# Dense work placed under the attention's exps by a build-time list schedule, with exps that carry no shift

## The chip, the cores and the metric

The kernel is one transformer block on one core of one Trainium2 chip. The metric is device time in microseconds of that core, the median of several executions. The engines are PE (matmul; PEld is its weight loading), ACT (activations), DVE (vector), POOL (GpSimd) and SP, which issues the DMAs. The program gives each engine its own instruction list in a fixed order, with semaphores between the lists.

## The reference

The block works on 2048 tokens of width 1024, in bf16: layer norm, attention with 32 heads of width 32, output projection, residual; then layer norm, a feed-forward layer of width 3584 with GELU, residual.

```python
def _A_ref(x, wqkv, wo):                       # attention
    q, k, v = ...(x @ wqkv)                    # 32 heads, Dh = 32
    p = softmax(einsum("bhqd,bhkd->bhqk", q, k) * Dh ** -0.5)
    return einsum("bhqk,bhkd->bhqd", p, v)... @ wo

def _B_ref(x, w1, b1, w2, b2):                 # feed-forward
    return gelu(x @ w1 + b1) @ w2 + b2         # tanh approximation

h  = x + _A_ref(layernorm(x), wqkv, wo)
h2 = h + _B_ref(layernorm(h), w1, b1, w2, b2)
```

## The kernel before

Three stages run one after the other: all projections; all attention; then, per chunk of 512 tokens, output projection, layer norm and feed-forward. In attention the scores of two heads, 128 keys and 512 queries form one "half unit": two matmuls of contraction 32 (row tiles of the PE array) into a 128x1024 score buffer in PSUM, and one exp of that buffer on ACT. For two half units together, four column tiles of PV and four of the denominator follow.

```python
NSTP = 2                                     # two score buffers
def stage_A(hu):                             # QK: two of four row tiles
    for j in range(2):
        hl = 2 * pr + j
        pe(matmul(sT[:, s, j, :], KT[32*hl:32*hl+32, g, kt*P:(kt+1)*P],
                  QT[32*hl:32*hl+32, g, qc*512:(qc+1)*512],
                  tile_position=(32 * hl, 0)), ...)
def stage_B(hu):                             # exp with a per-partition bias
    act(activation(PT[:, ps], sT[:, s], ACT.Exp, bias=biasm[:, g, qc:qc+1], scale=SCALE))
def stage_C(hu1):                            # four PV, then four denominator column tiles
    ...
for hu in range(NHU):                        # 1024 half units
    if hu + LA < NHU:
        stage_A(hu + LA); stage_B(hu + LA)
    if hu % 2 == 1:
        stage_C(hu); ...
# ... only then, chunk by chunk:
# output projection, layer norm, feed-forward (GELU by sigmoid on ACT)
```

`biasm` is an upper bound of the scores from row norms of Q and K: 64 squares on DVE, 64 matmuls with ones, 64 reductions. It keeps the exp's argument small.

Of the kernel before, what the change touches and what calls it, by code (L numbers as in the profile page):

```python
# [6 lines left out]
dt = mybir.dt  # L7
# [6 lines left out]


class Flow:

    def __init__(self, sem, eng, step=1):
        self.sem = sem
        self.eng = eng  # L20
        self.step = step
        self.count = 0
        self.pending = False

    def horizon(self):
        return self.value() + (self.step if self.pending else 0)

    def value(self):
        return self.count * self.step


class Buf:

    __slots__ = ("w", "r")

    def __init__(self):
        self.w = None
        self.r = {}


class Task:
    __slots__ = ("fn", "waits", "flow", "inc")

    def __init__(self, fn, waits, flow, inc):
        self.fn = fn
        self.waits = waits
        self.flow = flow
        self.inc = inc


class Plan:
    def __init__(self):
        self.tasks = {}
        self.main_flow = {}
        self.all_flows = []
        self.regions = []

    def register_flow(self, flow):
        self.all_flows.append(flow)
        return flow  # L60

    def track(self, space, lo, hi, bufs):
        deps = {}

        def merge(dep):
            if dep is None:
                return
            f, v = dep
            if deps.get(f, 0) < v:
                deps[f] = v  # L70

        for (sp, l, h, obufs) in self.regions:
            if sp == space and l < hi and lo < h:
                for ob in obufs:
                    merge(ob.w)
                    for f, v in ob.r.items():
                        merge((f, v))
        for b in bufs:
            for f, v in deps.items():
                if b.r.get(f, 0) < v:  # L80
                    b.r[f] = v
        self.regions.append((space, lo, hi, bufs))

    def add_engine(self, eng, flow):
        self.tasks[eng] = []
        self.main_flow[eng] = flow
        self.register_flow(flow)

    def task(self, eng, fn, reads=(), writes=(), flow=None, inc=True):
        if flow is None:  # L90
            flow = self.main_flow[eng]
        assert flow.eng == eng
        waits = {}

        def need(dep):
            if dep is None:
                return
            f, v = dep
            if v <= 0:
                return  # L100
            cur = waits.get(f)
            if cur is None or cur < v:
                waits[f] = v

        for b in reads:
            need(b.w)
        for b in writes:
            need(b.w)
            for f, v in b.r.items():
                need((f, v))  # L110
        if flow in waits and waits[flow] > flow.value():
            raise RuntimeError("same-engine dependency on a not-yet-incremented task; add inc=True")
        if inc:
            flow.count += 1
            flow.pending = False
            val = flow.value()
        else:
            flow.pending = True
            val = flow.value() + flow.step
        t = Task(fn, waits, flow if inc else None, inc)  # L120
        self.tasks[eng].append(t)
        for b in writes:
            b.w = (flow, val)
            b.r = {}
        for b in reads:
            old = b.r.get(flow)
            if old is None or old < val:
                b.r[flow] = val
        return t

    def emit(self, eng, eng_obj):
        waited = {}
        for t in self.tasks[eng]:
            for f, v in t.waits.items():
                if waited.get(f, 0) >= v:
                    continue
                eng_obj.wait_ge(f.sem, v)
                waited[f] = v
            ins = t.fn(eng_obj)
            if t.inc:  # L140
                ins.then_inc(t.flow.sem, t.flow.step)


class LNTemps:

    def __init__(self, SB, T, pfx, nslots, nbn, tiles=4):
        tq = tiles
        B = [Buf() for _ in range(nslots)]
        self.B = B

        def mk(name, shape, dtype):
            h, _ = SB(T, pfx + name, shape, dtype, bufs=B)
            return h

        self.stats = mk("stats", [P, nslots, tq, nbn * 6], dt.float32)
        self.mv = mk("mv", [P, nslots, tq, 2], dt.float32)
        self.mvb = mk("mvb", [P, nslots, tq, 2], dt.bfloat16)
        self.mvr = mk("mvr", [P, nslots, tq, 2], dt.float32)
        self.nm = mk("nm", [P, nslots, tq, 1], dt.float32)
        self.tb = mk("tb", [P, nslots, tq, 1], dt.bfloat16)  # L160
        self.y0 = mk("y0", [P, nslots, tq, 1], dt.float32)
        self.r0 = mk("r0", [P, nslots, tq, 1], dt.float32)
        self.q0 = mk("q0", [P, nslots, tq, 1], dt.float32)
        self.y1 = mk("y1", [P, nslots, tq, 1], dt.float32)
        self.denb = mk("denb", [P, nslots, tq, 1], dt.bfloat16)
        self.rden = mk("rden", [P, nslots, tq, 1], dt.float32)


class LanePool:

    def __init__(self, flows):
        self.flows = flows
        self.tokens = [Buf() for _ in flows]
        self.i = 0

    def next(self):
        k = self.i % len(self.flows)
        self.i += 1
        return self.flows[k], self.tokens[k]


def build_kernel(nc, A_x, A_wqkv, A_wo, B_w1, B_b1, B_w2, B_b2, out):
# [3 lines left out]
    H = D // DH  # L186
    assert D % P == 0 and S % 512 == 0 and F % P == 0 and H * DH == D
    NT = S // P
    NCH = S // 512
    DC = D // P  # L190
    G = DC
    FC = F // P
    OB = min(512, D)
    NVB = D // OB
    assert D % OB == 0
# [6 lines left out]
    out2 = out[0]  # L202

    plan = Plan()
    es = ExitStack()
    with es:
        T = es.enter_context

        def sem(name):
            return T(nc.semaphore(name))  # L210

        fpe = Flow(sem("f_pe"), E.PE)
        fact = Flow(sem("f_act"), E.Activation)
        fdve = Flow(sem("f_dve"), E.DVE)
        fpool = Flow(sem("f_pool"), E.Pool)
        fsp_dummy = Flow(sem("f_sp"), E.SP)
        plan.add_engine(E.PE, fpe)
        plan.add_engine(E.Activation, fact)
        plan.add_engine(E.DVE, fdve)
        plan.add_engine(E.Pool, fpool)  # L220
        plan.add_engine(E.SP, fsp_dummy)
        lanes_x = LanePool([plan.register_flow(Flow(sem(f"f_dx{i}"), E.SP, 16)) for i in range(3)])
        lanes_w = LanePool([plan.register_flow(Flow(sem(f"f_dw{i}"), E.SP, 16)) for i in range(6)])
        lanes_m = LanePool([plan.register_flow(Flow(sem(f"f_dm{i}"), E.SP, 16)) for i in range(2)])
        lanes_o = LanePool([plan.register_flow(Flow(sem(f"f_do{i}"), E.SP, 16)) for i in range(4)])

        def _flatten(x):
            if isinstance(x, Buf):
                return [x]
            out_ = []  # L230
            for y in x:
                out_ += _flatten(y)
            return out_

        def _mkbufs(shape):
            if shape is None:
                return Buf()
            if isinstance(shape, int):
                return [Buf() for _ in range(shape)]
            n, rest = shape[0], (shape[1] if len(shape) == 2 else shape[1:])  # L240
            return [_mkbufs(rest) for _ in range(n)]

        def SB(T_, name, shape, dtype, bufshape=None, bufs=None):
            h = T_(nc.sbuf_tensor(name, shape, dtype))
            m = nc.lookup_mloc(h)
            nbytes = mybir.dt.size(dtype)
            for d_ in shape[1:]:
                nbytes *= d_
            if bufs is None:
                bufs = _mkbufs(bufshape)  # L250
            plan.track("SB", m.addr, m.addr + nbytes, _flatten(bufs))
            return h, bufs

        def PSM(T_, name, shape, dtype, bufshape=None):
            h = T_(nc.psum_tensor(name, shape, dtype))
            m = nc.lookup_mloc(h)
            nbytes = mybir.dt.size(dtype)
            for d_ in shape[1:]:
                nbytes *= d_
            nbanks = (nbytes + 2047) // 2048  # L260
# [236 lines left out]
        def projections(tc, mid_hook=None):  # L497
# [12 lines left out]
            for jv in range(NVB):  # L510
                jb = (2 * D) // WBLK + jv
                s = load_wblock(jb)
                if jv == 0:
                    flush_tail()
# [381 lines left out]
```

## Time and profile before

| | before |
|---|---|
| median | 1880.46 us (3 runs); 1883.87 us with the run beside after |
| projections | 0 to about 244 us |
| attention | about 244 to 1353 us |
| output projection and feed-forward | about 1353 to 1887 us |

The page's second part cuts the span into 40 slices of 47 us. A digit is the busy share in tenths, and PEclk is the granted TensorE clock in tenths of full speed.

```profile
PE   4898989999999999999999999999868998999998
...
ACT  3433389999999999999999999999647137054150
...
PEclk9999955555555555555555555555579999999999
```

Two stages are PE's, at nearly full clock. The long stage between them is ACT's, and there the clock is half. The exps and QK matmuls among the groups. Columns: line, engine, operation, tiles, shapes and count; then busy us and mean ns of one; then idle time before them and what ended it.

```profile
L580 ACT ACTIVATE PT<-sT,biasm 128x1024 bf16<-128x1024 f32 x1024 | 1058.0, 1111 | 51.2 <-PE sT L569 51.2
L569 PE MATMUL sT<-QT,KT 32*128 32x512 bf16 x2048 | 593.3, 603 | 54.8 <-ACT PT L580 54.8
```

The timeline of before in attention, ACT alone and then PE alone, with start and length in us, count, and in brackets the wait before:

```profile
529.75 4.13 ACT L580 ACTIVATE PT<-sT,biasm 128x1024 bf16<-128x1024 f32 x4 [0.20 <-PE sT L569]
534.08 4.13 ACT L580 ACTIVATE PT<-sT,biasm 128x1024 bf16<-128x1024 f32 x4 [0.20 <-PE sT L569]
```

```profile
270.12 0.62 PE L597 MATMUL OTp<-PT,Vsb 128*32 128x512 bf16 x4
270.52 0.64 PE L605 MATMUL DENp<-PT,ones 128*32 128x512 bf16 x4
271.09 0.61 PE L569 MATMUL sT<-QT,KT 32*128 32x512 bf16 x2
271.90 0.60 PE L569 MATMUL sT<-QT,KT 32*128 32x512 bf16 x2 [0.20 <-ACT PT L580]
```

Four exps take 4.33 us from start to start of a run: 1.005 us each while they follow one another (three such steps and the last length of 1.11 make 4.13), and the rest is a wait for QK. At half clock the step from PV to denominator is 0.40 us, and from denominator to QK, where the tiling changes, 0.57.

The page's fourth part follows the chain of waits back from the last instruction:

```profile
PE 60%; ACT 19%; issue 15%; DVE 5%; DMA 0%; ACTq 0%; SPq 0%; DVEq 0%
PE sT L569 16%; ACT PT L580 16%; PE pb L782 10%; PE pb L752 8%; PE OTp L597 7%; PE DENp L605 6%; PE psq L438 5%; PE pb L694 3%; PE psv L483 3%; ACT xnb L379 2%; DVE l3stats L357 1%; PE pn L458 1%; DVE uu L762 1%; DVE l1stats L357 1%; DVE ost L797 1%
```

In attention the chain alternates between exp and QK: neither runs alone.

### The profile page before, as it was taken

The page shows a single profiled execution, that of the slowest core. Times are in us where ns is not written, and L with a number is a line of the kernel's source. Part 1 is how long each engine was busy: PE and PEld are TensorE (multiplying, and loading weights), DVE is VectorE, ACT ScalarE, POOL GpSimd, SP SyncE. Part 2 cuts the span into 40 slices and gives each one's busy share as a digit, 9 for nine tenths or more (in the row PEclk, how much of TensorE's full clock was granted, in tenths as well). Part 3 has the DMA queues.
Part 4 walks back from the last instruction along what each step waited for, and adds up shares of the span by engine and source line. Part 5 has one row for each costly group of instructions (what it writes and reads, how often), then busy time and mean ns, then how long its engine had stood idle before and what let it go on. Part 6 is the DMA issues. An engine that isn't in the chain of part 4 may idle for free.

```text
span 1886.6 us, 24076 instructions
## 1 busy us (share of the span) xinstructions
PE 1738.6 (92%) x9312; PEld 484.2 (26%) x9312; DVE 479.0 (25%) x849; ACT 1345.0 (71%) x1458; POOL 1.0 (0%) x9
## 2 busy tenths in 40 slices
PE   4898989999999999999999999999868998999998
PEld 2343411111111111111111111111133443444443
DVE  5454501010010010110100100100147147065271
ACT  3433389999999999999999999999647137054150
POOL 0000000000000000000000000000000000000000
PEclk9999955555555555555555555555579999999999
DMA  3443310000000000000000000000122533434434
GB/s 112 134 144 102 134 45 1 1 1 1 1 1 1 1 1 1 1 1 1 1 1 1 1 1 1 1 1 1 51 84 90 164 123 127 131 126 145 145 116 130
DMA packets 84176, 100.13 MB, mean 53 GB/s; under 512 B 7265, under 2 KB 64609, under 8 KB 84066
## 3 DMA queue, kind: packets, MB, share of 16 engines
q1 hardware_dynamic: 84066, 98.59, 16.3%
q8 instruction: 78, 1.28, 0.3%
q14 instruction: 32, 0.26, 0.0%
HBM read 94.38 MB, written 4.19 MB: 52 GB/s over the span
## 4 chain that ended last, share of the span: by engine, by line
PE 60%; ACT 19%; issue 15%; DVE 5%; DMA 0%; ACTq 0%; SPq 0%; DVEq 0%
PE sT L569 16%; ACT PT L580 16%; PE pb L782 10%; PE pb L752 8%; PE OTp L597 7%; PE DENp L605 6%; PE psq L438 5%; PE pb L694 3%; PE psv L483 3%; ACT xnb L379 2%; DVE l3stats L357 1%; PE pn L458 1%; DVE uu L762 1%; DVE l1stats L357 1%; DVE ost L797 1%
## 5 line engine op out<-in xcount | busy, mean ns | idle before, releaser
L580 ACT ACTIVATE PT<-sT,biasm 128x1024 bf16<-128x1024 f32 x1024 | 1058.0, 1111 | 51.2 <-PE sT L569 51.2
L569 PE MATMUL sT<-QT,KT 32*128 32x512 bf16 x2048 | 593.3, 603 | 54.8 <-ACT PT L580 54.8
L616 DVE RECIPROCAL rdenf<-DENp 128x512 f32<-128x512 f32 x32 | 107.4, 3358 | 990.9 <-PE DENp L605 990.9
L605 PE MATMUL DENp<-PT,ones 128*32 128x512 bf16 x2048 | 328.7, 633 | 0.0
L597 PE MATMUL OTp<-PT,Vsb 128*32 128x512 bf16 x2048 | 315.5, 607 | 0.4 <-ACT PT L580 0.4
L569 PEld LDWEIGHTS sT<-QT,KT 32*128 32x128 bf16 x2048 | 104.7, 99 | 711.0 <-ACT PT L580 710.5
L757 ACT ACTIVATE xh<-pb,b1f 128x512 bf16<-128x512 f32 x112 | 76.8, 686 | 217.6 <-PE pb L752 217.6
L752 PE MATMUL pb<-hnT,w1st 128*128 128x512 bf16 x896 | 213.2, 399 | 12.5 <-DVE ost L797 6.2
L782 PE MATMUL pb<-w2st,gT 128*128 128x512 bf16 x896 | 194.0, 379 | 0.0
L438 PE MATMUL psq<-xnT,wst 128*128 128x512 bf16 x512 | 128.9, 399 | 1.2 <-ACT xnT L395 1.2
L752 PEld LDWEIGHTS pb<-hnT,w1st 128*128 128x128 bf16 x896 | 90.4, 102 | 127.3 <-issue 27.4
L597 PEld LDWEIGHTS OTp<-PT,Vsb 128*32 128x32 bf16 x2048 | 57.3, 101 | 224.5 <-issue 223.2
L782 PEld LDWEIGHTS pb<-w2st,gT 128*128 128x128 bf16 x896 | 87.6, 98 | 105.8 <-issue 1.0
L739 ACT ACTIVATE th<-uu 128x512 bf16<-128x512 bf16 x112 | 69.9, 624 | 15.2 <-DVE uu L762 15.2
L762 DVE SCALAR_TENSOR_TENSOR uu<-sqf,xh 128x512 bf16<-128x512 bf16 x112 | 77.5, 692 | 3.9
L438 PEld LDWEIGHTS psq<-xnT,wst 128*128 128x128 bf16 x512 | 52.1, 102 | 66.9 <-issue 13.1
L797 DVE TENSOR_TENSOR ost<-pb,hch 128x512 bf16<-128x512 f32 x32 | 20.0, 685 | 190.3 <-PE pb L788 188.7
L694 PE MATMUL pb<-Wo,OT 128*128 128x512 bf16 x256 | 60.1, 392 | 4.2 <-DVE OT L617 4.2
L605 PEld LDWEIGHTS DENp<-PT,ones 128*32 128x32 bf16 x2048 | 64.0, 114 | 0.0
L760 DVE TENSOR_TENSOR sqf<-xh 128x512 bf16<-128x512 bf16 x112 | 46.9, 419 | 55.8 <-ACT xh L757 54.7
L483 PE MATMUL psv<-wst,xnT 128*128 128x512 bf16 x256 | 55.9, 379 | 0.0
L488 ACT ACTIVATE Vsb<-psv 128x512 bf16<-128x512 f32 x32 | 19.1, 597 | 43.0 <-PE psv L483 43.0
(66 smaller groups left out, 519.2 us busy)
## 6 DMA issues: line engine op xcount, KB each, us to landing
w1st<-in_B_w_dram SPq DMA_DIRECT2D x28, 1024.0 KB, 5.2
w2st<-in_B_w_dram SPq DMA_DIRECT2D x112, 256.0 KB, 2.6
wst<-in_A_wqkv_dram SPq DMA_DIRECT2D x24, 1024.0 KB, 4.9
xring<-in_A_x_dram SPq DMA_DIRECT2D x32, 256.0 KB, 3.2
out_dram<-ost SPq DMA_DIRECT2D x32, 128.0 KB, 1.7
Wo<-in_A_wo_dram SPq DMA_DIRECT2D x1, 2048.0 KB, 8.1
b2row<-in_B_b_dram SPq DMA_DIRECT2D x1, 2.0 KB
b1col_bf<-in_B_b_dram SPq DMA_DIRECT2D x1, 7.0 KB, 4.6
```

The lines of the kernel that those rows point to most:

```text
L438: pe(lambda p, dc=dc, b=b, s=s, cin=cin, xt=xt: p.matmul(psq[:, b, :], wst[:, s, dc, cin:cin + P], xnT[:, xt, dc, :], start=(dc == 0), sto ...
L483: pe(lambda p, dc=dc, t4=t4, s=s, pvs=pvs, xt=xt: p.matmul(psv[:, pvs, 0:OB], xnT[:, xt, dc, t4 * P:(t4 + 1) * P], wst[:, s, dc, :], start ...
L569: pe(lambda p, s=s, j=j, kt=kt, g=g, hl=hl, qc=qc: p.matmul(sT[:, s, j, :], KT[32 * hl:32 * hl + 32, g, kt * P:(kt + 1) * P], QT[32 * hl:3 ...
L580: act(lambda a, s=s, ps=ps, g=g, qc=qc: a.activation(PT[:, ps, :, :], sT[:, s, :, :], ACT.Exp, bias=biasm[:, g, qc:qc + 1], scale=SCALE), ...
L597: pe(lambda p, j=j, kt=kt, g=g, hl=hl, ps=ps, start=start, stop=stop, oi=oi: p.matmul(OTp[32 * hl:32 * hl + 32, oi, :], Vsb[:, kt, g * P + ...
L605: pe(lambda p, j=j, hl=hl, ps=ps, start=start, stop=stop, oi=oi: p.matmul(DENp[32 * hl:32 * hl + 32, oi, :], ones32[:, :], PT[:, ps, j, :] ...
L616: dve(lambda v, rs=rs, oi=oi: v.reciprocal(rdenf[:, rs, :], DENp[:, oi, :]), reads=[B_DENp[oi]], writes=[B_rdenf[rs]])
L694: pe(lambda p, sa=sa, g=g, qc=qc, t4=t4, j=j: p.matmul(pb[:, sa, 0:OB], OT[:, qc, g, t4 * P:(t4 + 1) * P], Wo[:, g, j * OB:(j + 1) * OB], ...
L752: pe(lambda p, hb=hb, s=s, dc=dc, f4=f4, hn=hn: p.matmul(pb[:, hb, :], w1st[:, s, dc, f4 * P:(f4 + 1) * P], hnT[:, hn, dc, :], start=(dc = ...
L757: act(lambda a, gs=gs, hb=hb, fc=fc: a.activation(xh[:, gs, :], pb[:, hb, :], ACT.Identity, bias=b1f[:, fc:fc + 1], scale=1.0), reads=[B_p ...
L762: dve(lambda v, gs=gs: v.scalar_tensor_tensor(uu[:, gs, :], sqf[:, gs, :], C2, xh[:, gs, :], ALU.add, ALU.mult), reads=[B_sqf[gs], B_xh[gs ...
L782: pe(lambda p, ci=ci, fc=fc, t4=t4, j=j, s2=s2: p.matmul(pb[:, ci, 0:OB], gT[:, fc, t4 * P:(t4 + 1) * P], w2st[:, s2, j * OB:(j + 1) * OB] ...
```

## The change

It has four parts.

1. The kernel is described as a graph of tasks with durations. A greedy list scheduler orders every engine's tasks at build time. On PE, QK goes first, PV when enough exps wait, and "background" (dense) matmuls fill the rest. Most of the projections, and output projection and feed-forward of chunks 0 to 2, become background of the attention stream.
2. The exp has no shift: the row norms and the bias pointer go. Inputs with larger scores were not tried.
3. QK issues four row tiles at once (two heads, two key tiles), with three score buffers instead of two. PV and denominator of one exp are four column tiles.
4. GELU uses tanh instead of sigmoid, and its first step leaves PSUM on DVE. In attention all background work shares one PSUM bank.

The diff has some 1,700 lines; this is its core, with cuts marked.

```diff
-            act(... ACT.Exp, bias=biasm[:, g, qc:qc + 1], scale=SCALE), ...
+                act(... ACT.Exp, bias=0.0, scale=SCALE), 1024, ..., kind="exp")
-    for hu in range(NHU): ...            # fixed order, stages in series
+    MM = 0.224                           # modelled us of a dense matmul
+    def schedule(self, pick_pe, switch=0.07, ...):   # list schedule
+        ...
+                    if e == E.PE:
+                        t = pick_pe(rd, now, state, up)
+                    else:
+                        t = min(rd, key=lambda x: (x.prio, num[x]))
+    def qk(self, qc, p16, r):
+        for half in range(2):
+            for j in range(2):
+                r0 = 64 * half + 32 * j
+                ... p.matmul(psum[:, 2 * us[half] + j, :], KT2[r0:r0 + 32, ...],
+                             QT2[r0:r0 + 32, ...], tile_position=(r0, 0))
+        pe(fns, 0.235, ..., kind="qk", mode="row")
+    def finish(self, qc, g, pr):          # softmax division on DVE
+        dve(... tensor_copy(Dsb, psum ...), prio=-1)
+        dve(... tensor_copy(Osb, psum ...), prio=-1)
+        ... reciprocal ..., prio=2)       # last in the choice on DVE
+    rest_of_projections()
+    attention_chunk(0, first=1)
+    for qc in range(1, NCH):
+        wo_ln2(R1, qc - 1, [7])           # background: PSUM bank 7 only
+        ffn1(R1, qc - 1, [7])
+        ffn2(R1, qc - 1, [7])
+        attention_chunk(qc)
+    ...                                   # last chunk: all eight banks
+    def pick_pe(rd, now, state, up):
+        if "qk" in best: return best["qk"]
+        if "pv" in best and (waiting >= PV_FORCE or ...): return best["pv"]
+        if "bg" in best: return best["bg"]
```

## The prediction

> **What bounds the kernel now.** The table of 40 slices shows three stages in series: projections (0 to about 248 us, TensorE clock mostly 0.94 to 1.0), attention (248 to about 1355 us, granted clock 0.50, ACT 9 tenths), output projection plus feed-forward (about 530 us, clock about 0.96, PE 9 tenths). In attention ACT is the limit: the groups view gives 1024 exps, 1058 us busy, 51 us idle; the timeline shows four exps in 4.13 us, then a 0.20 us wait for QK, 1.085 us each. PE looks 96% busy there, but with tiled matmuls at half clock. Outside attention ACT is half idle and PE is the limit.
>
> **What the change does.**
> 1. It moves dense matmuls under the exps: about 600 of the 768 projection matmuls, and three of four chunks of output projection and feed-forward (about 520 each), some 2160. At the timeline's 0.216 us (warm, dense) that is about 467 us.
> 2. It drops the row-norm bound (64 squares, matmuls, reductions) and the exp's bias pointer. The Trainium skill, "ScalarE: Activation LUTs", section "What ACT_TABLE_LOAD costs", gives 93 ns per pointer operand; the trace roughly agrees (512-wide activations 686 ns with bias, 597 to 624 without). Exp: 1.040 to about 0.947 us, 1024 of them 970 us. Tanh replaces sigmoid; that page has it in exp's table set, so table loads (1.28 us in the trace) vanish.
> 3. QK runs four tiles at once, with three score buffers instead of two. At full clock: about 0.22 us per two exps for QK, 0.43 for PV with denominator (estimates: half of the half-clock timeline).
> 4. It adds GELU evacuation on DVE (about 2.3 us per 512-wide tile, from 0.69, 0.42, 0.69, 0.69 us ops), one PSUM bank for all background work during attention[...], mode switches (0.11 to 0.14 us at half clock, estimated 0.07 to 0.1 at full), small GpSimd chains.
>
> **Critical path.** Lead-in about 70 us. Stream: ACT floor 1008 x 0.947 + 84 tanh x 0.53, about 1000 us; PE per two exps 0.22 + 0.43 + 4.3 x 0.216 + four switches, about 1.95 us, so 504 rounds also need about 1000 us. Two balanced limits in a fixed order will not overlap perfectly, and early in chunk 0 exps wait for K projections: I take 1085 us. Tail: last output projection 14, norm 12, first feed-forward layer 64 (28 x 2.3, DVE-bound), second 50, drains 15: 155 us. Sum 1310 us.
>
> **Prediction: 1310 us, 8 in 10 within 1225 to 1440.** Faster by over 2%: 0.95; same: 0.02; slower: 0.03.
>
> **What would show each step.** Exp mean near 1.02 us (0.09 below 1.111), start-to-start near 0.95 in steady stretches; granted clock in the stream above 0.8 instead of 0.50; ACT over 85% busy in the stream; exp's idle, mostly behind QK, 50 to 120 us; stream from 70 to about 1155 us; in the tail DVE over 90% busy during the first feed-forward layer.
>
> **What would make it wrong.** First, the clock. Tiled matmuls alone stayed at 0.50 although PE was 96% busy; dense ones got 0.95. I assume the mix is granted full clock. At half clock a round needs about 3.5 us of PE, the whole about 1950 us; half-time at half clock gives about 1550. Second, the build-time order: each engine is in order, so one mis-modelled duration (GpSimd chain, DVE behind a reciprocal, the single background bank) stalls QK and with it ACT. Third, background work not fitting under its chunk spills into the tail.

## The result

| | before | after |
|---|---|---|
| median (lowest to highest) | 1883.87 us (1880.23 to 1887.87) | 1271.72 us (1269.26 to 1273.60) |
| ratio of after to before | | 0.6746, 95% interval 0.6729 to 0.6764 |
| mean granted clock in the profile | 0.683 | 0.992 |
| last exp ends | about 1353 us | 1119 us |

A ratio here is the mean time of one kernel's runs over that of the other's of the same rounds, so it is not quite the ratio of the medians quoted. After is 32.5% faster, inside the predicted range. The outputs are right.

The slices of after (32 us each):

```profile
PE   5999998999998999999989999999899999996989
...
ACT  3777877999999999999999999999999999930220
...
PEclk9999999999999999999999999999999999997989
```

The clock is full nearly throughout, and PE and ACT are now busy at the same time. The exp's group:

```profile
L593 ACT ACTIVATE PT<-ps 128x1024 bf16<-128x1024 f32 x1024 | 969.3, 1034 | 51.6 <-PE ps L583 40.4
```

ACT reads as 97% busy in the stream (255.20 of 262 us below). One would say that ACT is the limit. The chain of waits says otherwise. First the window from 360 to 622 us, about one chunk (window, length, then busy us of PE, PEld, DVE, ACT, POOL, then clock, DMA share and GB/s), then the chain:

```profile
360.00:622.00 262.00, 242.90 (x2048) 71.67 (x2078) 141.60 (x219) 255.20 (x285) 8.52 (x28) 1.00 0.27 81
```

```profile
PE 67%; DVE 20%; ACT 5%; issue 4%; POOL 3%; DMA 1%; SPq 0%; POOLq 0%; DVEq 0%
PE ps L719 16%; PE ps L603 16%; PE ps L583 10%; PE ps L511 9%; PE ps L685 8%; ACT PT L593 4%; PE ps L660 3%; PE ps L552 3%; DVE a_xh L690 3%; DVE gT L698 2%; DVE Osb L617 2%; DVE Dsb L621 2%; DVE a_uu L694 2%; DVE Dsb L615 2%; DVE st L461 1%
```

The exp's share of the chain is 4%. The timeline shows why. First ACT in a stretch of second-layer background, then PE in one whole round of two exps:

```profile
544.83 15.53 ACT L593 ACTIVATE PT<-ps 128x1024 bf16<-128x1024 f32 x16 [0.23 <-PE ps L583]
```

```profile
513.07 0.40 PE L583 MATMUL ps<-QT_67,KT_65 32*128 32x512 bf16 x4
513.39 0.61 PE L719 MATMUL ps<-a_w2r,gT 128*128 128x512 bf16 x2
513.93 0.39 PE L603 MATMUL ps<-PT,V 128*32 128x512 bf16 x2
...
514.15 0.38 PE L603 MATMUL ps<-PT,V 128*32 128x512 bf16 x2
...
514.48 0.61 PE L719 MATMUL ps<-a_w2r,gT 128*128 128x512 bf16 x2
515.01 0.40 PE L583 MATMUL ps<-QT_67,KT_65 32*128 32x512 bf16 x4
```

Sixteen exps in 15.53 us with 1.02 us for the last are 0.967 us from start to start (the pitch). Successive activations overlap, so a wait of some 0.05 us between two of them hides inside the busy time. What ACT can do without waits shows in other runs below: 0.917 us. PE's round from QK to QK takes 1.94 us (515.01 - 513.07), with no wait: one QK pass, four dense matmuls, two PV passes. Two dense matmuls that follow one another, or two PV passes, are 0.215 us apart. Where the tiling changes, the step is 0.32 (513.07 to 513.39, and 514.15 to 514.48). So a change of tiling costs about 0.107 us, four of them 0.43 us, 22% of PE's round: 7 x 0.2155 + 4 x 0.107 = 1.94.

This reading is for the second layer's stretch. In the first layer's, where tanh runs between the exps, three exps in a row take 2.83 us (at 458.54 us), again about 0.917 from start to start, and ACT is busy for 39.0 of the 40 us from 440: there ACT itself is close to its limit. That PE's dense work sets the 0.967 is confirmed below: with less of it (a_thin_prio) the pitch in the second layer's stretch is 0.92.

The Trainium skill, "TensorEngine Tiling (Array Packing)", section "Key Properties", states that changing the tiling mode drains TensorE, without a size. In this trace the step is 0.107 us longer at each change. The same skill, "TensorE: Matmul & The Clock Gate", section "Wait — 56ns, not 53.3ns?", gives 215.7 ns between full-clock matmuls of 512 columns, and the 0.215 us here agrees.

### The profile page after: what moved, and what is told of

Its sections match the earlier page's. It is cut to its first block, busy times and chain, and to the rows that moved or that the text cites. A ratio compares the mean times of both kernels' runs of the same rounds, so it can differ in the third digit from the quotient of the medians.

```text
span 1267.5 us, 21571 instructions
## 1 busy us (share of the span) xinstructions
PE 1156.2 (91%) x9099; PEld 377.0 (30%) x9248; DVE 676.7 (53%) x1148; ACT 1052.7 (83%) x1174; POOL 67.3 (5%) x236
## 4 chain that ended last, share of the span: by engine, by line
PE 67%; DVE 20%; ACT 5%; issue 4%; POOL 3%; DMA 1%; SPq 0%; POOLq 0%; DVEq 0%
PE ps L719 16%; PE ps L603 16%; PE ps L583 10%; PE ps L511 9%; PE ps L685 8%; ACT PT L593 4%; PE ps L660 3%; PE ps L552 3%; DVE a_xh L690 3%; DVE gT L698 2%; DVE Osb L617 2%; DVE Dsb L621 2%; DVE a_uu L694 2%; DVE Dsb L615 2%; DVE st L461 1%
## 5 line engine op out<-in xcount | busy, mean ns | idle before, releaser
L593 ACT ACTIVATE PT<-ps 128x1024 bf16<-128x1024 f32 x1024 | 969.3, 1034 | 51.6 <-PE ps L583 40.4
L603 PE MATMUL ps<-PT,V 128*32 128x512 bf16 x2048 | 312.7, 384 | 25.7 <-DVE Osb L617 21.1
L607 PE MATMUL ps<-PT,ones_50 128*32 128x512 bf16 x2048 | 312.6, 385 | 0.0
L719 PE MATMUL ps<-a_w2r,gT 128*128 128x512 bf16 x848 | 239.8, 387 | 5.4 <-issue 4.9
L583 PE MATMUL ps<-QT_67,KT_65 32*128 32x512 bf16 x2048 | 202.3, 385 | 12.4 <-ACT PT L593 8.4
L685 PE MATMUL ps<-hnT,a_w1r 128*128 128x512 bf16 x630 | 166.8, 382 | 14.1 <-DVE a_xh L690 7.1
L511 PE MATMUL ps<-xnT,Wall 128*128 128x512 bf16 x478 | 128.3, 387 | 8.0 <-DVE stg L520 3.8
L603 PEld LDWEIGHTS ps<-PT,V 128*32 128x32 bf16 x2048 | 67.6, 94 | 202.8 <-issue 148.4
L621 DVE RECIPROCAL Dsb<-Dsb 128x128 f32<-128x128 f32 x128 | 113.7, 924 | 0.5
L719 PEld LDWEIGHTS ps<-a_w2r,gT 128*128 128x128 bf16 x896 | 69.3, 98 | 138.4 <-issue 98.4
```

The source lines that it names most:

```text
L511: pe(lambda p, dc=dc: p.matmul(psum[:, bank, :], Wall[:, blk, dc, c:c + P], xnT[:, tc, dc, :], start=(dc == 0), stop=(dc == DC - 1)), MM, ...
L583: return p.matmul(psum[:, 2 * us[half] + j, :], KT2[r0:r0 + 32, p16, tc, i, :], QT2[r0:r0 + 32, qs, pr, :], start=True, stop=True, tile_po ...
L593: act(lambda a, u=u, s=s: a.activation(PT[:, s, :, :], psum[:, 2 * u:2 * u + 2, :], ACT.Exp, bias=0.0, scale=SCALE), 1024, reads=[B_ps[2 * ...
L603: fns.append(lambda p, j=j, h=h: p.matmul(psum[32 * j:32 * j + 32, 6, :], V[:, kt, 32 * h:32 * h + 32], PT[:, s, j, :], start=first, stop= ...
L607: fns.append(lambda p, j=j: p.matmul(psum[64 + 32 * j:96 + 32 * j, 6, :], ones32[:, :], PT[:, s, j, :], start=first, stop=last, tile_posit ...
L621: dve(lambda v, k=k: v.reciprocal(Dsb[:, 128 * k:128 * k + 128], Dsb[:, 128 * k:128 * k + 128]), 0.9, reads=[B_Dsb[0][k], B_Dsb[1][k]], wr ...
```

## The experiments

Each kernel ran beside before on the same chip. The rounds were on several chips; before's median in them lies between 1882.64 and 1886.73 us, so a difference of a few us from after, which has a round of its own, is no finding. The labels that begin with a_ are variants of after, those with b_ variants of before.

### a_bias: the bias pointer back

```diff
-  ACT.Exp, bias=0.0, scale=SCALE)
+  ACT.Exp, bias=zb[:, 0:1], scale=SCALE)      # zb is a [128, 1] tile of zeros
```

> After, with the exp reading a zero bias through a per-partition pointer again; the build-time order is the same. Theory 1 (the stream is paced by ACT: 98% busy from 360 to 1118 us): each exp slot goes from 0.947 to 1.040 us, so about +80 to +95 us, 1350 to 1367 us, exp idle stays near 50 us. Rival (the stream is paced by PE, which reads 93% busy, and ACT only looks full): most of the longer exp is hidden, under +40 us, below 1310 us.

Measured: 1313.25 us, ratio 0.697 (0.6949 to 0.6992), about 42 us above after. That is just past the rival's limit (under 40 us, below 1310) and far from theory 1's 80 to 95. The chain tells why: first its shares by line in a_bias, then pieces of it (start, length and what) in a_bias and in after.

```profile
ACT PT L595 74%; PE ps L721 5%; ACT a_th L698 3%; PE ps L554 2%; PE ps L687 2%; PE ps L662 2%; PE ps L513 1%; PE ps L585 1%; PE ps L605 1%; DVE b_xh L692 1%; DVE gT L700 1%; DVE st L463 1%; ACT xnT L485 0%; DMA xr<-in_A_x_dram 0%; DVE b_uu L696 0%
```

```profile
516.56 151.68 ACT PT L595 x151
...
788.79 151.68 ACT PT L595 x151
```

```profile
647.03 6.53 ACT PT L593 x7
...
909.78 8.36 ACT PT L593 x9
```

With the pointer 151 exps take 151.68 us without a break: 1.005 us each, exactly before's pitch, and now the exps hold 74% of the whole chain instead of 4%. The two lines of a_bias are the same place in two chunks, 272.23 us apart; the two of after are 262.75 us apart. ACT's floor for a chunk with pointer is 256 x 1.005 + 28 tanh x 0.52 = 271.8 us, so a_bias loses nothing. Without pointer the floor is 256 x 0.917 + 28 x 0.51 = 249 us, and after misses it by 5%. PE's floor for a chunk is, estimated from the passes above, (128 QK + 256 PV + 520 dense) x 0.2155 + 512 changes x 0.107 = 250 us. After's two floors are equal, and the order loses 5% between them. With one clear limit it loses nothing. So dropping the pointer is worth 0.088 us per exp on ACT, but only 42 of about 90 us (1024 x 0.088) reach the total, because PE takes over. The Trainium skill, "ScalarE: Activation LUTs", section "What ACT_TABLE_LOAD costs", puts a pointer operand at about 93 ns; 0.088 us agrees roughly.

### b_nobias: the pointer alone, taken from before

```diff
-  ACT.Exp, bias=biasm[:, g, qc:qc + 1], scale=SCALE)
+  ACT.Exp, scale=SCALE)
```

> Before, with the exp's bias pointer removed and nothing else (row norms still computed). Theory 1 (before's attention is paced by ACT with PE at half clock just below): exp slot 1.040 to 0.947 us, but at half clock PE needs about 3.9 us per four exps (estimate from its timeline: four QK passes of 0.43, four PV or denominator passes of 0.43, four switches of 0.12), so it takes over as the limit near 3.95 us against 4.34: about -80 us, 1770 to 1830 us. Rival (PE at half clock already is the limit): within 20 us of before.

Measured: 1832.51 us, ratio 0.9718 (0.9696 to 0.974), 54 us below before, just past the end of the forecast. ACT's timeline:

```profile
522.75 3.77 ACT L580 ACTIVATE PT<-sT 128x1024 bf16<-128x1024 f32 x4 [0.38 <-PE sT L569]
526.90 3.77 ACT L580 ACTIVATE PT<-sT 128x1024 bf16<-128x1024 f32 x4 [0.38 <-PE sT L569]
```

The four exps shrink from 4.13 to 3.77 us, but the wait for QK grows from 0.20 to 0.38. A cycle is 4.15 us against 4.33, where 3.95 had been estimated. PE at half clock is nearly the limit in before, as theory 1 had it, with more overhead than assumed.

### a_serial: the same building blocks in series

```diff
+  # first QK of each attention chunk: after all earlier PE tasks
+  barrier = [t for t in gr.tasks if t.eng == E.PE] if (p16, r) == (first, 0) else ()
-  wo_ln2(R1, qc - 1, [7]); ffn1(...); ffn2(...)
+  wo_ln2(R1, qc - 1, [0, 1, 2, 3, 4, 5, 6, 7]); ffn1(...); ffn2(...)
```

> After, with the same tiles, buffers, exps and ops, but the first QK of each attention chunk ordered behind all earlier PE work, so that dense work and attention alternate instead of overlapping (dense work may use all free PSUM banks then). Theory 1 (the gain is the overlap): about 600 x 0.216 = 130 us of projections and three times about 145 us (the tail of after) come back: 1271 + 565 = about 1830 us, 1760 to 1870. The granted clock falls to about 0.5 in the attention stretches. Rival (the gain is the attention itself: four tiles at once, three buffers, no pointer): under 1650 us. If the clock stays near 1.0 in attention without dense work, then the new tiling, not the mix, keeps it up.

Measured: 1746.50 us, ratio 0.9259 (0.9234 to 0.9285). Serialising costs 475 us against after, so the overlap is the main gain. The remaining 140 us between before (1886.73 in these rounds) and a_serial is everything else in the change together (the new attention, no norms, tanh, the new order); this run does not separate it. The windows (columns as above): projections alone, then the first attention chunk alone.

```profile
100.00:205.00 105.00, 105.00 (x487) 47.45 (x485) 60.62 (x145) 0.00 (x0) 0.00 (x0) 1.00 0.22 71
205.00:430.00 225.00, 174.10 (x1441) 37.19 (x1440) 49.82 (x66) 221.08 (x240) 0.00 (x0) 0.65 0.04 13
```

```profile
329.72 29.49 ACT L593 ACTIVATE PT<-ps 128x1024 bf16<-128x1024 f32 x32 [0.27 <-PE ps L583]
```

The clock falls to 0.65 in attention without dense work, where about 0.5 was forecast. Yet 32 exps take 29.49 us, 0.918 us from start to start, so in attention the lower clock is no part of the 475 us. Before has 1.083 (4.33 / 4) at clock 0.50, and without its pointer 1.04 (4.15 / 4). The rest, to 0.918, comes from the new tiling, the third buffer and the somewhat higher clock, which this run does not separate. The total lies just below the forecast of 1760 to 1870, whose centre of 1830 added the dense work to after's own stream. Alone the exps run at 0.918 us instead of after's 0.967, which makes about 50 of the 84 us (1024 x 0.049, an estimate); the rest is open.

### b_fill_dense, b_fill_col, b_fill_one: what lifts the clock

Useless matmuls on real data are put into before's attention, into the output bank that is idle:

```diff
+  if kt >= 3:
+      other = 1 - oi
+      for rep in range(2):                     # b_fill_one: range(1)
+          # b_fill_dense: one full matmul
+          pe(matmul(OTp[:, other], Vsb[:, kt, 0:128], KT[:, g, 512*rep:512*rep+512]))
+          # b_fill_col, b_fill_one: the same as four column tiles of 32
+          for hl in range(4): pe(matmul(OTp[32*hl:32*hl+32, other], ..., tile_position=(0, 32*hl)))
```

> Before, with two useless dense matmuls (full 128x128 weights, 512 columns) after each pair of attention half units from the fourth key tile on, into the output bank that is idle then. Theory 1 (the clock is granted by dense work in the mix): the attention clock goes from 0.50 to above 0.9; PE then needs about 1.6 us per two exps and ACT stays the limit: within 3% of before (1830 to 1900 us), although PE got 800 more dense matmuls. Rival (any tiled share keeps it at half): the clock stays 0.50, PE needs about 2.9 us per two exps, about 2200 us.

> The same filler as the dense one in time and data, but each dense matmul cut into four column tiles of 32, as PV is. Theory 1 (what counts is dense work): clock stays 0.50 and PE becomes the limit, about 2.9 us per two exps, about 2200 us. Rival (what counts is how full PE is, whatever the tiles): the clock rises above 0.9 as with the dense filler and the time stays within 3% of before.

> Before with half of the column-tiled filler (one set instead of two per pair). It places the clock between before (0.50) and the full filler (0.93). If the clock is granted while PE is saturated and taken back when it is not, PE swings: at half clock one set saturates it (about 2.6 us per two exps against 2.17), at full clock it does not: mean clock in attention 0.65 to 0.9. If any saturation at half clock is enough to keep it: above 0.9. Time within 3% of before under both.

Measured: b_fill_dense 1898.10 us (ratio 1.0073, 1.0054 to 1.0091), b_fill_col 1870.28 (0.992, 0.9901 to 0.9939), b_fill_one 1868.51 (0.9927, 0.9904 to 0.9951). The same stretch in before, b_fill_dense, b_fill_col and b_fill_one, in that order:

```profile
400.00:700.00 300.00, 286.04 (x1666) 47.70 (x1664) 36.43 (x18) 286.15 (x278) 0.00 (x0) 0.50 0.00 1
```

```profile
400.00:700.00 300.00, 257.30 (x1837) 63.98 (x1870) 32.39 (x16) 283.14 (x275) 0.00 (x0) 0.91 0.00 1
```

```profile
400.00:700.00 300.00, 260.45 (x2604) 67.91 (x2600) 36.44 (x18) 289.77 (x283) 0.00 (x0) 0.93 0.00 1
```

```profile
400.00:700.00 300.00, 248.79 (x2148) 60.15 (x2146) 36.45 (x18) 287.94 (x282) 0.00 (x0) 0.80 0.00 1
```

Theory 1, that only dense work is granted the clock, falls: column tiles lift it as well (0.50 to 0.93), and half as many lift it to 0.80. The forecast for b_fill_one holds: PE swings, with clocks of 0.54, 1.00, 1.00, 1.00, 0.67, 0.90, 0.95 and 0.50 in the eight windows of 4 us from 700 us on.

So added work lifts the clock, dense or in column tiles. The profile's busy share does not show it: before reads higher (about 95%) than b_fill_one (83%) at 0.80. The number of passes does not either: before's attention has two per exp, 1.85 per us (278 exps in 300 us), a_serial's only 1.6 (1.5 per exp, 240 in 225 us), and a_serial has the higher clock. But before's QK fills two of four row tiles. Counted as half a pass, with the filler at 13 of 16 key tiles, the order fits: before 1.4 full passes per us, a_serial 1.6, b_fill_one 1.8, b_fill_dense 2.1, b_fill_col 2.2, with clocks of 0.50, 0.65, 0.80, 0.91 and 0.93. This is an estimate from the counts, made afterwards; no run tests it. With the filler, before does more work and takes 0.8% less time. The dense filler costs more than the tiled one; it adds changes of tiling, and this was not tested apart.

### b_nobias_fill: does the clock then help before?

The edits of b_nobias and b_fill_col together:

```diff
-  ACT.Exp, bias=biasm[:, g, qc:qc + 1], scale=SCALE)
+  ACT.Exp, scale=SCALE)
+  for rep in range(2): ...               # column-tiled filler, as above
```

> Before without the exp's bias pointer and with the useless column-tiled filler. Theory 1 (without the pointer, PE at half clock was the limit, 97 us of exp idle; more PE work lifts the clock above 0.9 and so removes it): exp idle under 50 us, 1765 to 1795 us, that is, 40 to 65 us below the same kernel without filler (1832.5). Rival (the added work costs PE time as usual): 1832 us or more.

Measured: 1823.49 us, ratio 0.9675 (0.9648 to 0.9701) against 0.9718 without filler, on another chip. The clock rose to about 0.94 in attention, but the exp's idle time fell only from 97 to 77 us. The exp's group in b_nobias, then in b_nobias_fill:

```profile
L580 ACT ACTIVATE PT<-sT 128x1024 bf16<-128x1024 f32 x1024 | 965.4, 1021 | 97.5 <-PE sT L569 97.5
L580 ACT ACTIVATE PT<-sT 128x1024 bf16<-128x1024 f32 x1024 | 963.7, 1029 | 77.1 <-PE sT L569 75.9
```

Theory 1 falls, and the total is 9 us below the rival's 1832 as well. The filler stands in the fixed order before the next QK; whether that is what keeps the waits was not tested.

### a_thin and a_thin_prio: less background work

In the stream of chunks 1 to 3 every background contraction is cut to a quarter. The result is wrong on purpose.

```diff
-  for dc in range(DC):        # first layer; output projection and second layer likewise
+  nd = DC if len(banks) > 1 else 2
+  for dc in range(nd):
```

> After, wrong on purpose: in the stream of chunks 1 to 3 every output projection and feed-forward contraction is cut to a quarter (about 1.1 dense matmuls per two exps instead of 4.3); evacuations, exps and the last chunk are kept. Theory 1 (ACT paces the stream): the stream of chunks 1 to 3 shortens by under 3% (it cannot go below about 1008 x 0.947 + tanh), whole -10 to -40 us, 1230 to 1262 us, if the clock stays. Rival (PE paces it): nothing faster is possible on ACT, so again little; what tells more is the clock: if it is granted by PE being busy it falls towards 0.5 in chunks 1 to 3 and stays 1.0 in chunk 0; if one dense matmul per round is enough, it stays near 1.0.

Measured: 1406.95 us (ratio 0.7466, 0.7452 to 0.7481), 135 us slower than after, with less work. No theory had this. The clock fell too, so the tempting story is that the cold PE holds the stream. The windows of a_thin, one in the first feed-forward layer and one after it, and ACT's timeline in the first:

```profile
400.00:450.00 50.00, 18.18 (x36) 2.42 (x38) 43.09 (x75) 11.24 (x19) 0.00 (x0) 0.50 0.32 94
500.00:550.00 50.00, 35.95 (x328) 8.22 (x324) 13.22 (x18) 49.66 (x56) 0.00 (x0) 0.76 0.25 79
```

```profile
404.25 1.23 ACT L697 ACTIVATE a_th<-a_uu 128x512 f32<-128x512 bf16 x2 [4.09 <-DVE a_uu L695]
```

At 500 us the clock is 0.76 and ACT is 99% busy: the clock is not the cause. At 400 us DVE is 86% busy and ACT runs nothing but tanh. No exp runs from 382.9 to 464.9 us, 82 us, and in the two later chunks 62 us each. With so few matmuls the first layer is limited by DVE. Between GELU steps (priority 1) and softmax reciprocals (priority 2) the scheduler always takes GELU, so the copies that would free the output accumulator, PV, the score buffers and the exps all stand. The trace shows it: three of a group's four reciprocals start by 378.44 us, and the fourth only at the end of the layer (in the later chunks the gap is as long, 685 to 763 and 989 to 1067 us):

```profile
457.35 0.95 DVE L621 RECIPROCAL Dsb<-Dsb 128x128 f32<-128x128 f32 x1
```

This reading was tested by changing two numbers:

```diff
-  ... reciprocal ..., prio=2)
+  ... reciprocal ..., prio=0)          # and the product after it
```

> The thinned kernel (1407 us) with one edit: the softmax reciprocals and the product after them get the first place instead of the last in the build-time choice on DVE. Theory 1 (thinning made the first feed-forward layer DVE-bound; in that stretch the order puts its GELU ahead of the reciprocals, the output accumulator is not freed and the exps stand still for about 45 us in each of three chunks): the ACT gaps vanish, 1255 to 1285 us. Rival (the exps stood still because the clock fell to 0.5 there): the gaps stay, over 1380 us. The clock in chunks 1 to 3 stays near 0.7 under either.

Measured: 1258.33 us (ratio 0.6681, 0.6662 to 0.6701). The gaps are gone (theory 1): 149 us from two priorities. The windows of a_thin_prio around the same place, in the first layer and after it:

```profile
360.00:450.00 90.00, 67.10 (x574) 17.01 (x574) 77.88 (x129) 86.40 (x102) 8.86 (x28) 0.87 0.35 98
450.00:622.00 172.00, 136.41 (x1187) 34.63 (x1187) 75.78 (x117) 169.65 (x189) 7.83 (x28) 0.83 0.29 90
```

The clock is still only 0.83 to 0.87, and ACT is 96 to 99% busy. In the second layer's stretch 62 exps take 57.23 us, 0.92 us from start to start, against 0.967 in after:

```profile
478.23 57.23 ACT L593 ACTIVATE PT<-ps 128x1024 bf16<-128x1024 f32 x62 [0.15 <-PE ps L583]
```

Even so, a_thin_prio gains only some 13 us over after, although three quarters of that dense work are gone. After itself with the new priorities was not run, so how these 13 us divide between the two edits is open.

### a_mm_slow: the same instructions, scheduled with a wrong duration

```diff
-    MM = 0.224
+    MM = 0.43
```

> After, with the dense matmul's duration in the build-time model set to 0.43 us (half clock) instead of 0.224; the same instructions, another order. Theory 1 (the order is only as good as its durations): about half of the dense work is placed under the exps, PE idles in the stream, some 800 dense matmuls spill into the tail or into stretches of stalled exps: 1400 to 1500 us. Rival (any greedy interleave does, the queues and buffers even it out): within 30 us of after.

Measured: 1564.25 us (ratio 0.8299, 0.8285 to 0.8313), 293 us above after, more than forecast. Theory 1 holds in direction and place; its size was too small. In the stream the exps run near 0.917 us (64 in 58.77 us from 268.65 on). Then they stand still at each change of chunk:

```profile
ACT PT L593 <- PE ps L607: 196.7, 3, 67.7
```

Three stops of up to 67.7 us, 197 us together. The chain through the first of them (438 to 500 us) runs over the remaining projections, the output projection and the layer norm of the chunk before. The attention output has a single buffer, so a chunk cannot deliver its first heads before the output projection of the chunk before has read them: background that is late stops the stream. Only what is late in the last chunk can spill. From the last exp (1336.6 us) to the end are 227 us instead of after's 149, with 197 records of the second layer of the chunk before still to come between 1337 and 1391 us (34 in after from 1119 us on). The three stops and the longer tail make 275 of the 293 us.

### a_tailact and a_best: the tail

In the last chunk ACT has no exps, so the first layer's evacuation goes there:

```diff
+  if len(banks) > 1:                    # last chunk
+      act(activation(xh, psum[:, bank], ACT.Identity, bias=b1f[:, fc:fc+1]))
+  else: dve(tensor_scalar(xh, psum[:, bank], b1f[:, fc:fc+1], None, ALU.add))
```

> After, with the first feed-forward layer's evacuation of the last chunk on ACT instead of DVE (0.75 us of 2.5 us per tile leaves DVE). Theory 1 (DVE, busy 52 of 57 us, paces that layer): it takes about 50 us, paced by 224 x 0.216 = 48 us of PE, so -5 to -9 us, 1262 to 1267 us. Rival (PE paces it, 52 of 57 us busy too): within 2 us of after.

Measured: 1261.67 us, ratio 0.6691 (0.6676 to 0.6706), 10 us below after. The first layer of the last chunk in after and in a_tailact:

```profile
1156.00:1213.00 57.00, 51.90 (x225) 22.86 (x229) 51.96 (x91) 13.29 (x22) 0.00 (x0) 0.95 0.32 93
```

```profile
1156.00:1206.00 50.00, 50.00 (x225) 22.26 (x224) 44.22 (x79) 32.06 (x53) 0.00 (x0) 0.96 0.36 106
```

In after PE and DVE both read 52 of 57 us. Taking work from DVE gives 50 us with PE at 50.00, so DVE was the limit (theory 1).

a_best adds the output projection of the last chunk in the order of token tiles, so that layer norm starts earlier:

```diff
-  for j in range(2):
-      for t4 in range(4): ...            # all eight groups, then four norms
+  for t4 in range(4):
+      for j in range(2): ...
+      norm(t4)                           # last chunk only
```

> After, with the last chunk's feed-forward evacuation on ACT (as measured, 1262 us) and, in the last chunk only, the output projection in the order of token tiles, so that the layer norm of a tile starts after its own two halves and not after all eight groups. Theory: the 13 us in which PE ran 4 us between output projection and feed-forward shrink to about 5, and PE is not cooled down: -6 to -11 us, 1250 to 1256 us. Rival (the layer norm chain itself sets it): within 3 us of 1262.

Measured: 1260.86 us, ratio 0.6699 (0.6685 to 0.6712): no difference from a_tailact. PE still runs only 4.4 us between 1143 and 1156 us, because the built order puts the residual adds of the last two tiles behind the norms of the first two (at 1142.60 us in its timeline; this reason was read there, not tested). a_tailact stands as the version that beats both kernels.

## Why the prediction was right, point by point

- **Total**: 1310 us, range 1225 to 1440, against 1271.72. Right, 3% high.
- **Overlap is the gain**: shown. Undoing it alone (a_serial) gives back 475 of 612 us.
- **Clock**: predicted above 0.8 in the stream, measured 1.00. The worry that tiled matmuls are kept cold was misplaced (b_fill_col); what lifts the clock instead is not settled. That the overlap needs the full clock follows from PE's round, which has no wait at 1.94 us; no run at half clock with full background shows it.
- **Two balanced limits near 1000 us**: right in kind. PE's round was put at 1.95 us and takes 1.94, with 4 dense matmuls where 4.3 were assumed and changes of tiling at 0.107 where 0.07 to 0.1 was assumed; the two deviations cancel, so the match to 0.01 is luck. ACT's pitch was put at 0.947 us: ACT alone does 0.917, and in the stream PE holds it to 0.967. The old pitch of 1.040 is not from the trace either: busy time over count gives 1.033, the timeline 1.005; 1.040 is what the last section works out from the skill's page.
- **The mis-sized term**: lead-in 70 plus stream 1085 gave 1155 us for the end of the exps, and 1119 was measured, 36 of the 38 us of error. The allowance of 85 us for imperfect overlap and early waits was too large for the predicted limit of 1000 us: from 70 us on the stream took 1049. Against a limit at ACT's measured pitch (1008 x 0.917 + 84 x 0.51 = 967) the allowance would have fit, so it and the too slow pitch cannot be judged apart. Exp idle was 51.6 us (50 to 120 forecast), and in the chunks shown the loss is 5%.
- **Pointer**: the 93 ns mechanism holds (0.088 us measured), but its worth in after is 42 us, because PE is as long.
- **Tail**: 155 us predicted, about 149 measured (1119 to 1267.5). DVE was 91% busy in its first layer, as forecast, and a_tailact confirms the limit. The parts fit less well: the four DVE ops listed sum to 2.49 us, not 2.3, and GELU ran from 1156 to 1225 us, 69 us instead of 64; the second layer had begun by then, at 1212.8.
- **Fixed order as a danger**: shown by a_mm_slow (+293 us from one wrong duration) and by a_thin (+149 us from two priorities). Here the model's durations fit, and it did not bite.

## What to carry to other kernels

Where two stages have opposite limits, running one under the other is worth the shorter of them, but the sum of each engine's work per round must be counted, changes of tiling included. Read a limit from the pitch and the chain, not from the busy share: an ACT that was 97% busy was being paced by PE for much of the stream. A build-time order is as good as its durations and priorities; the long, rare task that frees a buffer should not stand last in them.

## What the Trainium skill lacked or had wrong

- "TensorE: Matmul & The Clock Gate", Part 1, has the clock halved when PE idles and full after some 3.4 us of busy work. It does not say what counts as busy. Before's attention stayed at 0.50 for 1.1 ms with PE read as about 95% busy; added column tiles raised it to 0.93, half as many to 0.80; a_serial's attention, with four row tiles at once, had 0.65. The measure itself stays open.
- "TensorEngine Tiling (Array Packing)", "Key Properties", gives no size for the drain at a change of tiling: about 0.107 us at full clock here, 0.43 of a 1.94 us round.
- "ScalarE: Activation LUTs", "What ACT_TABLE_LOAD costs": 186 or 280 ns plus 0.833 ns per element, less 93 ns of overlap, would make a 1024-wide exp 0.946 us without and 1.040 with pointer. Measured from start to start: 0.917 and 1.005.
- "Trainium Kernel Development and Optimization", "Best Practices", has occupancy as a fine measure for engines other than PE. Overlapping activations hid a 5% wait in an ACT that read 97% busy.
